# A third buffer for output rows, and an input check finished one turn earlier, in a fused attention and state-space kernel

## The chip, the cores and the metric

The kernel runs on one core of a Trainium2 chip. A core has a matrix engine (TensorE, PE in the profile; its weight loads are listed apart as PEld), a vector engine (VectorE, DVE), a scalar engine for activations and copies (ScalarE, ACT), a general engine (GpSimd, POOL) and a queue for transfers (SyncE, SP). Each works through its own instructions in order, and they wait for one another by semaphores. Matrix products are written to PSUM, from which VectorE and ScalarE read. The metric is the device time of one execution in microseconds; less is better.

## The reference

Two blocks follow each other. The first is a gated linear attention that is written as a recurrence over time: a state of 48 x 48 per head decays by alpha, takes up an outer product of k and v, and is read with q. The second projects the result with `w_in` to a value and a gate, runs a first-order recurrence over the values, multiplies by the gate's SiLU, and projects with `w_out`.

```
state = alpha[:, :, t, :, None] * state + einsum('bhd,bhe->bhde', k[:, :, t], v[:, :, t])
y[:, :, t] = einsum('bhd,bhde->bhe', q[:, :, t], state)          # B=4, H=8, S=768, D=48
x = y.transpose(0, 2, 1, 3).reshape(B, S, H * D)                 # (4, 768, 384)
val, gate = split(x @ w_in)                                      # 512 each
h = a * h + val[:, t]                                            # a = exp(A_log)
out = (silu(gate) * hs) @ w_out                                  # (4, 768, 384), float32
```

The weights and `A_log` arrive as 64-bit floats, and the kernel works in 32-bit floats.

## The kernel before, in words

The sequence is cut into N = 12 groups of 256 steps (three to each of four batches). The function `fast` writes out the order of all instructions by hand: in the loop over turns `n`, a turn projects group n and does the attention of group m = n + 1, while VectorE already prepares later groups. The order of each engine's instructions is the order in which they are written; nothing is rescheduled.

The parts of a turn, with their lines:

- `scores` (L792) and `masks` (L807, L808, L810): products of scaled keys and queries, and their causal mask.
- `values` (L826), `states` (L858), `carried` (L839): what a group's own steps give, the state that it adds, and what earlier states give. `join` (L952 to L957) copies the result out of PSUM and moves it by transfers into `xT`.
- `project(n, cc)` (L976): six products for one quarter of the inner width, three for the value (`pv`), then three for the gate (`pg`); each is carried out as two passes of 256 columns, so a projection is twelve entries in the profile. VectorE then scans `pv` into `hh` (L983), ScalarE makes the gate `sg` from `pg` (L994), and POOL, in the first two turns and in the last one VectorE, multiplies them (L996).
- `output(n)` (L1010): eight products of the gated values with `w_out`, and for each half an eviction by ScalarE into a row `o_sb` (L1004) and a transfer to memory (L1005). Outputs of turns 0 and 1 both fall in turn 1, those of turns 2 to 10 at the end of their own turn, and the last one behind a branch (L1262 to L1270).
- `products` (L661 to L678), advanced step by step by `go`: VectorE's preparation of a later group, with the transposes (L600), the long scans P (L635) and V (L654), and the scaled keys and queries (L619, L610).

Matrix results of `scores` (one half), `project` and `output` live in four PSUM buffers named `mm`, one bank each. Which of the four a tile gets is settled when the program is built: the planner behind the pools simulates the program and gives out a buffer when, by its own estimate, the tile that held it has been read for the last time. It then adds the semaphore waits that the choice requires. `bank("s0")` and its kin are further banks with one buffer each. The rows `o_sb` come from a pool of their own, `rows`, in SBUF.

The kernel has a range check. For inputs outside the range that its method can handle, a second function, `general`, computes the whole again. `check_w(i)` (L567) takes the largest and smallest magnitude of one of six weight parts, `check_end` (L574 to L583) joins these with what was collected on alpha into a column `okc` of 128 ones or zeros, and `check_flag` sums that column by a product with ones on TensorE into the bank `s0` (L587) and makes the flag from it (L589, L590). All engines read the flag at the end of the last turn (L1234) and branch (L1255).

Of the kernel before, what the change touches and what calls it, by code (L numbers as in the profile page):

```python
# [346 lines left out]
def fast(  # L347
# [30 lines left out]
    N = B * NG  # L378
# [67 lines left out]
    NW = 6  # L446
# [491 lines left out]
    for h in range(H):  # L938
        i, e, s = h // 4, h % 4 // 2, h % 2 ^ h // 4
# [23 lines left out]
    def project(n, cc, late=False, between=None):  # L963
        if cc == 0:
            if n == 0:
                fs[n] = [wide[:, k // 2, ds(k % 2 * GC, GC)] for k in range(NI)]
            else:
                fs[n] = [f_last[:, k] for k in range(NI)]
        xT = xTs[n]
        pv, pg = [t[:, 0:GC] for t in bank_pair()]  # L970
        order = [(vg, kk) for vg in range(2) for kk in range(NK)]
        if n == 0 and cc == 0:
            order.sort(key=lambda x: x[1])
        def passes(part):
            for vg, kk in part:
                nc.tensor.matmul((pv, pg)[vg], w_ins[cc][:, kk, vg, :], xT[:, kk, :],  # L976
                                 start=(kk == 0), stop=(kk == NK - 1))

        passes(order[:NK] if between else order)
        hh = p2.tile([C, GC], FP32, tag=f"h{cc}", name="hh")  # L980

        def scan():
            nc.vector.tensor_tensor_scan(  # L983
                out=hh, data0=a_dec[:, cc:cc + 1].to_broadcast([C, GC]), data1=pv,
                initial=prev_h[cc][:, GC - 1:GC] if n % NG else 0.0, op0=ALU.mult, op1=ALU.add)
            prev_h[cc] = hh

        if not late:
            scan()
        if between:  # L990
            between()
            passes(order[NK:])
        sg = gates.tile([C, GC], FP32, tag="sg", name="sg")
        nc.scalar.activation(sg, pg, AF.Silu)  # L994
        engine = nc.vector if n < 2 or n == N - 1 else nc.gpsimd
        f = lambda: engine.tensor_mul(fs[n][cc], sg, hh)  # L996
        return (scan, f) if late else f
# [33 lines left out]
    def go(count):  # L1031
        for _ in range(count):
            next(steps, None)
# [75 lines left out]
    for n in range(N):  # L1109
        m = n + 1  # L1110
        if n == 0:
            V = scan_V(1, P)
            high(1)
            fs_late = [project(n, 0)]
            add_low(1)
            alphas(2)
            scaled_k(1, tk, V)
            scaled_q(1, tq, P)
            low(2)
            fs_late.append(project(n, 1))  # L1120
            convert(2)
            first(m)
            tk = straighten(2, "k")
            P = scan_P(2)
            tq = straighten(2, "q")
            V = scan_V(2, P)
            low(3)
            convert(3)
            load_raw("k", 3, nc.sync)
            junk(1)  # L1130
            def across_and_states():
                values(m, True)
                add_banks(m, states(m))

            f2 = project(n, 2, between=across_and_states)
            nc.scalar.activation(wobits[0][0:1, 0, 0, 0:1], minus[0:1], AF.Relu)
            load_w_out(0, nc.sync)
            alphas(3)
            third(m)
            load_w_out(1, nc.sync)  # L1140
            for name in "qa":
                load_raw(name, 3 + (name == "a"), nc.sync)
            load_v(3, nc.sync)
            for c in range(G):
                scaled_k(2, tk, V, c)
                scaled_q(2, tq, P, c)
        elif n == 1:
            scores(m)
            masks(m)
            h3, f3 = project(0, 3, True)  # L1150
            f2()
            P = scan_P(3)
            h3()
            values(m, True)
            st = states(m)
            add_banks(m, st)
            for f in fs_late:
                f()
            f3()
            f0 = project(n, 0)  # L1160
            convert(4)
            junk(2)
            low(5)
            convert(5)
            f1 = project(n, 1)
            f0()
            tk = plain("k")
            turn("k", tk)
            third(m)
            load_raw("k", 4, nc.sync)  # L1170
            load_v(4, nc.sync)
            f1()
            junk(3)
            V = scan_V(3, P)
            f2 = project(n, 2)
            scaled_k(3, tk, V)
            f2()
            output(0)
            f3 = project(n, 3)
            tq = plain("q")  # L1180
            turn("q", tq)
            load_raw("q", 4, nc.sync)
            scaled_q(3, tq, P)
            f3()
            go(1)
        else:
            if n == 2:
                first(m)
            if n - 1 not in late:
                second(m)  # L1190
                go(4)
            else:
                go(1)
            f0 = project(n, 0)
            f0()
            if n == 2:
                go(2)
            load_raw("k", n + 3, nc.sync)
            load_raw("a", n + 3, nc.sync)
            go(1)  # L1200
            f1 = project(n, 1)
            f1()
            if n - 1 in late:
                second(m)
            if n == 4:
                go(1)
            if n == N - 2:
                for i in range(0, 2):
                    check_w(i)
            go(1)  # L1210
            f2 = project(n, 2)
            f2()
            if n == N - 2:
                check_w(2)
            if n == N - 1:
                check_flag()
            if n != 4:
                go(1)
            load_raw("q", n + 3, nc.sync)
            f3 = project(n, 3)  # L1220
            f3()
            third(m)
            if n not in late:
                first(m + 1)
            elif n > 2:
                go(3)
            load_v(m + 2, nc.sync)
        if n == N - 2:
            for i in range(3, NW):
                check_w(i)  # L1230
            check_end()
        if n == N - 1:
            tc.mark_branch_hint_location("last", hint=0, engines=[mybir.EngineType.PE, mybir.EngineType.Activation, mybir.EngineType.DVE, mybir.EngineType.SP, mybir.EngineType.Pool])
            value = nc.values_load(flag[0:1, 0:1], min_val=0, max_val=1)  # L1234
        if 0 < n < N - 1:
            output(n)
        if n > 1 and n in late:
            first(m + 1)
# [3 lines left out]
@with_exitstack  # L1242
def kernel(ctx: ExitStack, tc: tile.TileContext, *args):
    nc = tc.nc
    out = args[-1]
    C, GC, NI = 128, 256, 4
    B, S, DM = out.shape
    keep = ctx.enter_context(tc.tile_pool(name="keep", bufs=1))
    ps_mm = ctx.enter_context(tc.tile_pool(name="ps_mm", bufs=4, space=bass.MemoryType.PSUM))
    w_outs = [keep.tile([C, 2, DM], FP32, name=f"w_out{i}") for i in range(2)]  # L1250
    f_last = keep.tile([C, NI, GC], FP32, name="f_last")
    rows = ctx.enter_context(tc.tile_pool(name="rows", bufs=2))
    with tc.manual_schedule():
        good = fast(tc, *args, w_outs, f_last, ps_mm, rows)
    with tc.If(good <= 0, preferred_fallthrough_block=True, label="last") as choice:  # L1255
        general(tc, *args, w_outs)
    with choice.Else(), tc.manual_schedule():
        half = DM // 2
        for c, at, size in ((0, 0, DM), (1, 0, half), (1, half, half)):
            o = ps_mm.tile([C, 512], FP32, tag="mm", name="mm")[:, 0:size]  # L1260
            for cc in range(NI):
                nc.tensor.matmul(o, f_last[:, cc, ds(c * C, C)], w_outs[cc // 2][:, cc % 2, ds(at, size)],  # L1262
                                 start=(cc == 0), stop=(cc == NI - 1))
            if not at:
                o_sb = rows.tile([C, DM], FP32, tag="o_sb", name="o_sb")
            if c and not at:
                nc.vector.tensor_copy(out=o_sb[:, 0:half], in_=o)
            else:
                nc.scalar.activation(o_sb[:, ds(at, size)], o, AF.Copy)
            nc.scalar.dma_start(out=out[B - 1, ds(S - GC + c * C, C), ds(at, size)], in_=o_sb[:, ds(at, size)])  # L1270
# [30 lines left out]
```

## Time and profile before

| what | value |
|---|---|
| median of 3 runs | 276.58 us (276.08 to 277.28) |
| the profiled execution | 276.15 us |
| its span, from first to last instruction | 274.4 us |
| TensorE busy | 269.5 us, 98% of the span |
| VectorE busy | 217.7 us, 79% |
| ScalarE busy | 109.6 us, 40% |
| POOL busy | 123.8 us, 45% |
| granted TensorE clock | 1.00 |

A row of a timeline reads: start in us from the span's start, duration, engine, line of the kernel, operation, output <- inputs, shapes, number of instructions; in brackets the idle time of that engine just before, and what ended it. A row of the chain gives start, duration and line of a piece of the work that ended last. A row of the waits reads: who, for whom, us in total, times, longest. A row of groups reads: line, operation, shapes, count, busy time, mean ns of one, idle time of the engine before them. Matrix products are pipelined, so their durations overlap and their spacing is shorter than one duration.

### The profile page before, as it was taken

How to read it: one execution, taken by the hardware profiler on the slowest of the kernel's cores; microseconds unless marked ns; L12 is line 12 of the kernel's file. 1: busy time of each engine (PE TensorE's matmuls, PEld its weight loads, DVE VectorE, ACT ScalarE, POOL GpSimd, SP SyncE). 2: the span in 40 equal slices, each digit the busy share in tenths (PEclk: the TensorE clock that was granted, in tenths of full speed). 3: DMA queues.
4: the chain of work that ended last, by engine and by line, in shares of the span. 5: the costliest groups of instructions: out<-in, count | busy, mean ns of one | idle time of the engine just before them, and what ended most of it. 6: DMA issues, size and time to landing. Idle time of an engine off the chain costs nothing.

```text
span 274.4 us, 9649 instructions
## 1 busy us (share of the span) xinstructions
PE 269.5 (98%) x4060; PEld 216.9 (79%) x4060; DVE 217.7 (79%) x271; ACT 109.6 (40%) x252; POOL 123.8 (45%) x144
## 2 busy tenths in 40 slices
PE   8999999999999999999999999999999999999995
PEld 6988888877788687788688688688687787786874
DVE  6979998996798999694995995996995992179440
ACT  3668766451344333523434424425425415213211
POOL 8122223260137485385384485376366476325000
PEclk9999999999999999999999999999999999999999
DMA  6937985989639686774677595586596501201101
GB/s 188 319 113 221 304 182 160 256 172 230 168 92 227 163 189 152 199 170 116 153 183 155 149 210 136 142 202 144 137 210 146 137 0 36 70 0 42 63 5 60
DMA packets 52303, 41.18 MB, mean 150 GB/s; under 512 B 27392, under 2 KB 50944, under 8 KB 52256
## 3 DMA queue, kind: packets, MB, share of 16 engines
q1 hardware_dynamic: 49328, 37.34, 54.2%
q0 software_dynamic: 1536, 2.20, 2.9%
q10 hardware_dynamic: 1392, 0.99, 1.2%
q8 instruction: 33, 0.54, 0.9%
q14 instruction: 14, 0.11, 0.1%
HBM read 32.54 MB, written 4.72 MB: 136 GB/s over the span
## 4 chain that ended last, share of the span: by engine, by line
PE 91%; DVE 5%; issue 1%; ACT 1%; POOL 1%; DVEq 0%; POOLq 0%; ACTq 0%
PE mm L976 46%; PE mm L1010 21%; PE y L826 4%; PE y L839 4%; PE mm L792 3%; PE s L792 3%; PE s L858 3%; PE mm L1262 2%; DVE P L635 2%; PE mm L701 1%; PE y L773 1%; DVE V L654 1%; POOL w_in L556 1%; PE s L717 1%; DVE Zk L619 0%
## 5 line engine op out<-in xcount | busy, mean ns | idle before, releaser
L976 PE MATMUL mm<-xT,w_in 128*128 128x256 f32 x576 | 129.7, 382 | 0.1
L976 PEld LDWEIGHTS mm<-xT,w_in 128*128 128x128 f32 x576 | 107.9, 190 | 16.2 <-POOL w_in L556 0.4
L1010 PE MATMUL mm<-w_out,f_last 128*128 128x384 f32 x160 | 54.2, 492 | 0.0
L994 ACT ACTIVATE sg<-mm 128x256 f32<-128x256 f32 x48 | 18.4, 383 | 86.1 <-PE mm L976 86.0
L996 POOL TENSOR_TENSOR f_last<-sg,hh 128x256 f32<-128x256 f32 x36 | 33.0, 918 | 33.5 <-ACT sg L994 17.7
L1010 PEld LDWEIGHTS mm<-w_out,f_last 128*128 128x128 f32 x160 | 29.7, 190 | 19.8
L878 POOL TENSOR_TENSOR sum<-sum,dS 128x192 f32<-128x192 f32 x30 | 30.3, 1010 | 21.5 <-ACT dS L866 11.8
L983 DVE TENSOR_TENSOR_SCAN hh<-a_dec,hh,mm 128x256 f32<-128x256 f32 x32 | 23.4, 731 | 16.1 <-PE mm L976 16.1
L635 DVE TENSOR_TENSOR_SCAN P<-al,lower 128x1028 f32<-128x1028 f32 x12 | 31.4, 2618 | 0.5
L654 DVE TENSOR_TENSOR_SCAN V<-al,ends 128x1028 f32<-128x1028 f32 x12 | 28.3, 2360 | 0.4
L955 POOL DMA_DIRECT2D xT<-yst x44 | 22.5, 517 | 12.5 <-ACT yst L952 11.2
L1004 ACT ACTIVATE o_sb<-mm 128x384 f32<-128x384 f32 x22 | 10.8, 490 | 37.3 <-issue 21.2
L810 POOL TENSOR_TENSOR AK<-AK,mask 128x512 f32<-128x512 f32 x9 | 15.2, 1684 | 18.7 <-ACT AK L808 18.7
L807 DVE TENSOR_TENSOR A<-s,mask 128x256 f32<-128x256 f32 x9 | 3.8, 425 | 19.5 <-PE s L792 19.5
L556 POOL TENSOR_TENSOR w_in<-w_in,wr 128x768 int32<-128x768 int32 x4 | 7.3, 1822 | 25.9 <-DVE wr L551 16.1
L600 DVE STREAM_TRANSPOSE k<-raw_k 128x1024 f32<-128x1024 f32 x9 | 18.3, 2035 | 0.0
L600 DVE STREAM_TRANSPOSE q<-raw_q 128x1024 f32<-128x1024 f32 x9 | 18.2, 2021 | 0.0
L600 DVE STREAM_TRANSPOSE al<-raw_a 128x1024 f32<-128x1024 f32 x8 | 16.3, 2038 | 0.0
L619 DVE TENSOR_TENSOR Zk<-k,V 128x1024 f32<-128x1024 f32 (+1 forms) x14 | 16.1, 1150 | 0.1
L826 PEld LDWEIGHTS y<-AK,v 64*64 64x64 f32 x352 | 12.1, 134 | 5.1 <-issue 5.1
L610 DVE TENSOR_TENSOR Zq<-q,P 128x1024 f32<-128x1024 f32 (+1 forms) x14 | 14.8, 1060 | 0.1
L826 PE MATMUL y<-A,v 64*64 64x64 f32 x352 | 14.5, 221 | 0.0
(163 smaller groups left out, 389.7 us busy)
## 6 DMA issues: line engine op xcount, KB each, us to landing
v<-in_v_dram SPq DMA_DIRECT2D x22, 192.0 KB, 3.3
out_dram<-o_sb SPq DMA_DIRECT2D x22, 192.0 KB, 2.2
raw_k<-in_k_dram SPq DMA_DIRECT2D x18, 184.0 KB, 3.7
raw_q<-in_q_dram SPq DMA_DIRECT2D x18, 184.0 KB, 3.8
raw_k<-in_k_dram SPq DMA_DIRECT2D x18, 176.0 KB, 3.9
raw_q<-in_q_dram SPq DMA_DIRECT2D x18, 176.0 KB, 4.0
wbits<-in_moe_w_in_dram SPq DMA_DIRECT2D x8, 384.0 KB, 5.3
raw_a<-in_alpha_dram SPq DMA_DIRECT2D x16, 184.0 KB, 4.9
```

The source lines that it names most:

```text
L600: nc.vector.transpose(out=by_runs(to).rearrange("p h c j -> p h j c"), in_=raws[name][:, 0:4 * ROW].rearrange("p (h j d) -> p h j d", h=4, ...
L635: nc.vector.tensor_tensor_scan(out=P, data0=al[:, 0:4 * GP], data1=lower.rearrange("p h t -> p (h t)"), initial=0.0, op0=ALU.mult, op1=ALU ...
L654: nc.vector.tensor_tensor_scan(out=V[:, ::-1], data0=al[:, 1:4 * GP + 1][:, ::-1], data1=ends.rearrange("p h t -> p (h t)")[:, ::-1], init ...
L792: nc.tensor.matmul(scs[m][c][i][ds(L * h, L), ds(p * (L + D), L + D)], Zk[rows, c, p, ds(h * L, L)], Zq[rows, u, p], start=True, stop=True ...
L826: nc.tensor.matmul(ys[m][i][ds(64 * s, 64), e, ds(c * C + h * L, L)], v_sb[rows, c, 4 * i + p, :], As[i][rows, c, p, :], start=across and ...
L878: nc.gpsimd.tensor_add(Ss[j][:, :, 0:D], Ss[j - 1][:, :, 0:D], part)
L955: engines[n % len(engines)].dma_start(out=xT[to, a], in_=st[rows, i, e])
L976: nc.tensor.matmul((pv, pg)[vg], w_ins[cc][:, kk, vg, :], xT[:, kk, :], start=(kk == 0), stop=(kk == NK - 1))
L983: nc.vector.tensor_tensor_scan(out=hh, data0=a_dec[:, cc:cc + 1].to_broadcast([C, GC]), data1=pv, initial=prev_h[cc][:, GC - 1:GC] if n % ...
L994: nc.scalar.activation(sg, pg, AF.Silu)
L996: f = lambda: engine.tensor_mul(fs[n][cc], sg, hh)
L1010: nc.tensor.matmul(os[c], fs[n][cc][:, ds(c * C, C)], w_outs[cc // 2][:, cc % 2, :], start=(cc == 0), stop=(cc == NI - 1))
```

## The change

Three things are changed. The pool `rows` gets three buffers instead of two. In the last turn but one (n = N - 2 = 10), the reductions of the range check move: four of the six weight parts stand ahead of the turn's first projection, one behind the second, one behind the third, and the end of the check behind the fourth; before, two parts stood behind the second projection, one behind the third, and three with the end of the check behind the attention. The summing product of the check moves from the third projection of the last turn to the end of turn 10, directly in front of that turn's output, and its two VectorE instructions with it.

```
             else:
                 go(1)
+            if n == N - 2:
+                for i in range(4):
+                    check_w(i)
             f0 = project(n, 0)
             f0()
...
             if n == N - 2:
-                for i in range(0, 2):
-                    check_w(i)
+                check_w(4)
             go(1)
             f2 = project(n, 2)
             f2()
             if n == N - 2:
-                check_w(2)
-            if n == N - 1:
-                check_flag()
+                check_w(5)
             if n != 4:
                 go(1)
             load_raw("q", n + 3, nc.sync)
             f3 = project(n, 3)
             f3()
+            if n == N - 2:
+                check_end()
             third(m)
...
         if n == N - 2:
-            for i in range(3, NW):
-                check_w(i)
-            check_end()
+            check_flag()
         if n == N - 1:
...
-    rows = ctx.enter_context(tc.tile_pool(name="rows", bufs=2))
+    rows = ctx.enter_context(tc.tile_pool(name="rows", bufs=3))
```

The built programs hold the same instructions on every engine. On TensorE only the summing product changes its place; on VectorE the check's instructions do; the order on ScalarE, POOL and SP is the same. The semaphore waits differ in more places.

More of the change, by code (lines that the diff above doesn't have):

```diff
@@ L1193, in fast @@
                 go(1)
+            if n == N - 2:
+                for i in range(4):
+                    check_w(i)
             f0 = project(n, 0)
@@ L1207, in fast @@
             if n == N - 2:
-                for i in range(0, 2):
-                    check_w(i)
+                check_w(4)
             go(1)
@@ L1213, in fast @@
             if n == N - 2:
-                check_w(2)
-            if n == N - 1:
-                check_flag()
+                check_w(5)
             if n != 4:
@@ L1221, in fast @@
             f3()
+            if n == N - 2:
+                check_end()
             third(m)
@@ L1228, in fast @@
         if n == N - 2:
-            for i in range(3, NW):
-                check_w(i)
-            check_end()
+            check_flag()
         if n == N - 1:
@@ L1251 @@
     f_last = keep.tile([C, NI, GC], FP32, name="f_last")
-    rows = ctx.enter_context(tc.tile_pool(name="rows", bufs=2))
+    rows = ctx.enter_context(tc.tile_pool(name="rows", bufs=3))
     with tc.manual_schedule():
```

## The prediction

> **What bounds the kernel now.** I read the busy shares first, then the groups of instructions for what TensorE waited, then the chain that ended last, and last the stretches the edit touches, instruction by instruction.
>
> ```profile
> span 274.4 us, 9649 instructions
> ...
> PE 269.5 (98%) x4060; PEld 216.9 (79%) x4060; DVE 217.7 (79%) x271; ACT 109.6 (40%) x252; POOL 123.8 (45%) x144
> ...
> L976 PE MATMUL mm<-xT,w_in 128*128 128x256 f32 x576 | 129.7, 382 | 0.1
> ...
> L1010 PE MATMUL mm<-w_out,f_last 128*128 128x384 f32 x160 | 54.2, 492 | 0.0
> ```
>
> TensorE works for 269.5 of 274.4 us, and its two costliest lines waited 0.1 and 0.0 us in all. No other engine can be made faster to any effect; what counts is whether TensorE gets an instruction more or less, or a wait it does not have now. The chain around the second turn, the place that matters below:
>
> ```profile
> 66.62 5.16 PE mm L1010 x16
> 71.78 0.93 PE s L792 x32
> 72.71 0.77 PE mm L792 x32
> 73.48 5.38 PE mm L976 x24
> 78.85 0.62 PE y L826 x32
> ...
> 86.43 0.47 PE y L839 x32
> 86.90 0.09 issue
> 86.99 1.00 PE s L792 x32
> ```
>
> Every piece is TensorE's own work and starts where the one before ended; the only wait is 0.09 us at 86.90.
>
> **The change, part by part.**
>
> *Third row buffer, for the rows themselves: 0.* It lets an eviction start before the transfer of the row two evictions earlier has landed. The closest two outputs are those of turns 0 and 1, both evicted in turn 1:
>
> ```profile
> 64.97 2.09 SPq L1005 DMA_DIRECT2D out_dram<-o_sb  x2
> 71.22 0.49 ACT L1004 ACTIVATE o_sb<-mm 128x384 f32<-128x384 f32 x1 [4.18 <-PE mm L1010]
> ...
> DMA to landing us min/median/max: 1.6/2.0/4.2
> ```
>
> The first row left at 64.97 and landed at the latest 4.2 us on, at 69.2; its buffer is wanted again at 71.22, and that eviction waited for TensorE's L1010. Elsewhere a whole turn lies between two outputs. So no eviction waits for a row.
>
> *Third row buffer, for the PSUM banks: +2.0.* The diff does not tell this; the built programs do. The four PSUM buffers named mm are given out, when the program is built, in the order in which the planner thinks they come free, and that order changes when two evictions no longer wait for a row. The instructions of turn 2's first projection, with what each waits for (before, then after; the pv group is the first three, the pg group the next three):
>
> ```
> L976 Matmult mm<-xT,w_in_93 128x256 [waits DMAHW0_49,DMASW1_49,DMASW0_49]
> L976 Matmult mm<-xT,w_in_93 128x256 [waits Activation_49]
> L976 Matmult mm<-xT,w_in_93 128x256 x2
> ...
> L976 Matmult mm<-xT,w_in_93 128x256 [waits DMAHW0_49,DMASW1_49,DMASW0_49]
> L976 Matmult mm<-xT,w_in_93 128x256 [waits DVE_49]
> L976 Matmult mm<-xT,w_in_93 128x256 x2
> ```
>
> Before, pg's first matmul waits for ScalarE: the eviction of a row, long over. After, it waits for VectorE, for the count of the scan L983 that reads pv of this same projection: pv and pg have been given one and the same bank (their PSUM addresses are equal, the only such pair among the 163 mm tiles). So pg cannot begin until VectorE has scanned pv. When is that? VectorE's order is unchanged here, and the scan stands behind the long scan P:
>
> ```profile
> 73.53 0.42 DVE L807 TENSOR_TENSOR A<-mm,mask 128x256 f32<-128x256 f32 x1 [0.34 <-PE mm L792]
> 73.87 2.29 DVE L635 TENSOR_TENSOR_SCAN P<-al,lower 128x1028 f32<-128x1028 f32 x1
> 76.07 0.72 DVE L983 TENSOR_TENSOR_SCAN hh<-a_dec,hh,mm 128x256 f32<-128x256 f32 x1
> ```
>
> The mask product, itself waiting for TensorE's L792, ends at 73.9, P runs until 76.1, the scan until 76.07+0.72 = 76.79. TensorE, in its rows, starts pg's first pass (the seventh of the 24) at 74.81:
>
> ```profile
> 74.81 0.38 PE L976 MATMUL mm<-xT,w_in 128*128 128x256 f32 x1
> ...
> 246.93 0.73 POOL L996 TENSOR_TENSOR f_last<-sg,hh 128x256 f32<-128x256 f32 x1 [2.50 <-DVE hh L983]
> ...
> L976 PE MATMUL mm<-xT,w_in x364: 379/379/483, 99.8 to 247.9; 128*128 128x256 f32 x182
> ```
>
> From VectorE's end to the waiter's start no TensorE wait of this kind is in the trace. The nearest row is POOL's at 246.93, behind a scan that ended at 246.05+0.74 = 246.79 (row further down): 0.14. The other end is 0. I take 0.05, as the weight load itself carries the wait and nothing stands before it. A first pass after a stop takes 483 instead of 379 ns, as that row's largest and smallest show: 0.10. The stall is 76.79+0.05-74.81+0.10 = 2.13 us; its ends are 1.98 (nothing for either) and, with P at its slowest, 2.97:
>
> ```profile
> 213.19 3.04 DVE L635 TENSOR_TENSOR_SCAN P<-al,lower 128x1028 f32<-128x1028 f32 x1
> ```
>
> (76.79+0.14-74.81+0.10 = 2.22, and 3.04-2.29 = 0.75 more). What stands behind the held instruction is all of TensorE's queue, so everything later moves by the same amount. VectorE and POOL gain slack, so the 0.09 us at 86.90 goes: net +2.04. The other groups of turn 2 whose waits changed name readers that are over by then: ScalarE's copies of the masks' step (before L858), and a scan that ends at 82.50+0.74 = 83.24 (row below), for pv of the turn's fourth projection. TensorE reaches that one at 80.20+2.7 = 82.9 by the profile of before (the second L976 pair of the turn starts behind L826 and L858, at 78.85+0.62+0.72 = 80.2), and some 2.1 us later, at 85.0, after.
>
> ```profile
> 82.50 0.74 DVE L983 TENSOR_TENSOR_SCAN hh<-a_dec,hh,mm 128x256 f32<-128x256 f32 x1
> ```
>
> *Range check earlier: 0, under cover of TensorE, if the check is in time.* In turn 10 VectorE now does four pairs of reductions ahead of the first scan, one pair behind the second, one behind the third, and the end of the check behind the fourth.
>
> ```profile
> 231.13 0.42 DVE L807 TENSOR_TENSOR A<-mm,mask 128x256 f32<-128x256 f32 x1 [0.34 <-PE mm L792]
> 239.37 0.75 DVE L983 TENSOR_TENSOR_SCAN hh<-a_dec,hh,mm 128x256 f32<-128x256 f32 x1 [7.81 <-PE mm L976]
> 241.96 0.75 DVE L983 TENSOR_TENSOR_SCAN hh<-a_dec,hh,mm 128x256 f32<-128x256 f32 x1 [1.84 <-PE mm L976]
> 242.62 0.93 DVE L567 TENSOR_REDUCE wmax<-wbits 128x1 f32<-128x768 f32 x1
> ...
> 246.05 0.74 DVE L983 TENSOR_TENSOR_SCAN hh<-a_dec,hh,mm 128x256 f32<-128x256 f32 x1
> ...
> 254.20 0.18 DVE L574 TENSOR_SCALAR rok<-ratio 128x48 f32<-128x48 f32 x1
> ...
> 255.10 0.16 DVE L583 TENSOR_REDUCE okc<-ok 128x1 f32<-128x4 f32 x1
> ```
>
> Four reductions take 246.05-242.62 = 3.43, one 0.86. Eight of them fit from 231.55 to 238.4, ahead of the scan at 239.37. TensorE's pace then brings scans every 2.59: 239.37, 241.96, 244.55, 247.14; a pair of 1.72 fits between each two. In turn 10 the last two scans even come earlier than now (the third at 244.55 instead of 246.05), which moves POOL's products forward and nothing on TensorE. The check's end, 254.20 to 255.26, is 1.06 long and would run from 247.8 to 248.9.
>
> *The summing product (L587) in front of the output: -0.2.* It waits for okc, and all of L1010, the output of turn 10, is queued behind it, and behind that turn 11.
>
> ```profile
> 249.81 1.56 PE L1010 MATMUL mm<-w_out,f_last 128*128 128x384 f32 x4
> ...
> 263.01 0.12 PE s L587 x2
> ...
> 260.52 0.38 ACT L994 ACTIVATE sg<-mm 128x256 f32<-128x256 f32 x1 [2.21 <-PE mm L976]
> 263.11 0.38 ACT L994 ACTIVATE sg<-mm 128x256 f32<-128x256 f32 x1 [2.21 <-PE mm L976]
> 266.01 0.38 ACT L994 ACTIVATE sg<-mm 128x256 f32<-128x256 f32 x1 [2.52 <-PE mm L976]
> ```
>
> TensorE gets there at 249.81, 0.9 us after okc; turn 2's shift moves both alike. Where L587 stands now it costs more than its own 0.12: the gates of turn 11 come 2.59 apart without it (260.52 to 263.11) and 2.90 with it (263.11 to 266.01), so 0.31; the weights of L976, else loaded ahead, are loaded in the open behind it. In front of L1010 that load is in the open already, since the small tiles of L839 go before; there I take its own 0.12, with 0.31 as the other end. Net 0.12-0.31 = -0.19 (ends -0.19 and 0). The two VectorE instructions behind it (L589, L590) and the reading of the flag by all engines come some 13 us earlier; nothing waited for them on TensorE, so 0.
>
> **Sum.** +2.13 -0.09 -0.19 = +1.85 us. The profiled execution took 276.15 us (span 274.4), so 278.00; the median of the runs shown is 276.58, 0.43 above it, and I carry the same difference: 278.4, +0.67%. With the ends: 1.98-0.09-0.19 = 1.70 to 2.97, so 278.3 to 279.6, and the runs before spread over 276.08 to 277.28, so about half a microsecond more to either side. What a measurement of this kernel can tell from no change is 0.5%, 1.4 us.
>
> **Rivals.** *The stall is swallowed further on* (the other side: not slower). Place: a later point where TensorE waits for a transfer or another engine in any case; price: the stall up to that point's idle time. From 0.7 us on it would decide against "slower" (1.85-0.7 is under 1.4). Then 276.58-0.19 = 276.4. Against it: after 64 us no wait is put down to TensorE's matmuls at all, and its weight loads show, in the waits from 64 us to the end, only these:
>
> ```profile
> PEld y L826 <- issue: 4.5, 9, 0.5
> PEld y L839 <- issue: 3.0, 9, 0.3
> PEld s L792 <- PE mm L1010: 1.1, 2, 0.5
> ```
>
> They come alike in every turn, at changes of tile shape, with matmuls running meanwhile. Chance 0.08.
>
> *The flag's product becomes the bound.* If one pair of reductions ran past its scan, okc would come 1.7 us later, at 250.6, and L587 would hold the output for 250.6-249.8 = 0.8 us: 278.4+0.8 = 279.2. It decides from 0.9 us of delay on. For it: the gaps between scan and pair are only 0.2 us wide. Chance 0.06.
>
> *The clock falls in the stall.*
>
> ```profile
> 268.00:271.00 3.00, 3.00 (x18) 2.65 (x16) 0.36 (x1) 0.49 (x1) 0.00 (x0) 1.00 0.19 68
> 271.50:274.40 2.90, 0.00 (x0) 0.00 (x0) 0.00 (x0) 0.00 (x0) 0.00 (x0) 1.00 0.11 34
> ```
>
> The seventh figure behind the stretch's length is the granted clock: 1.00 at work, and 1.00 still over 2.9 us without a matmul at the end. A stall of 2 us should leave it. If it halved for one projection of 2.59 us, the time would be 278.4+2.6 = 281.0. Chance 0.04. [...]
>
> *Faster by more than 0.5%*: would need the evictions' waits to be TensorE's, with 3.3 us to win; L1010's 0.0 speaks against it. Chance 0.02.
>
> **Chances and range.** The stall of about 2 us, alone: 0.80, own range 277.6 to 279.6. With the late flag, 0.86 is held by 277.5 to 279.8; the swallowed stall and the fallen clock are left out. Slower by over 0.5% (above 278.0): most of the first case (0.73), the late flag and the clock, 0.83. Within 0.5%: the swallowed stall, and the part of the first that spread hides, 0.15. Faster: 0.02.
>
> **What would show it.** A pause on TensorE of about 2 us at 74.8, ended by VectorE's hh (L983), before the seventh L976 of turn 2; L792 of that turn at about 89.0 instead of 86.99, with no wait before it; L1010 of turn 10 some 2.2 us later than 249.81, the gates of turn 11 all 2.59 apart, L587 right before L1010 with no wait for okc; the clock at 1.00. The prediction is wrong if no pause stands at 74.8, or if the shift shrinks between turns 3 and 10.

## The result, and the profile after

The changed kernel takes 279.29 us in the median of 8 runs (277.55 to 279.95); the kernel before, measured beside it, takes 276.42 us (275.83 to 277.28, 8 runs). The ratio is 1.0091, with a 95% interval of 1.0063 to 1.0119: slower by about 0.9%. The profiled execution of the changed kernel took 279.95 us.

The page of the changed kernel, first its busy shares and the granted clock over 40 slices of the span, then the groups of its two costliest lines:

```profile
span 278.2 us, 9640 instructions
...
PE 271.4 (98%) x4060; PEld 218.2 (78%) x4060; DVE 220.1 (79%) x271; ACT 109.6 (39%) x252; POOL 124.5 (45%) x144
...
PEclk9999999999979999999999999999999999999999
...
L976 PE MATMUL mm<-xT,w_in 128*128 128x256 f32 x576 | 131.4, 386 | 2.0 <-DVE hh L983 1.9
...
L1010 PE MATMUL mm<-w_out,f_last 128*128 128x384 f32 x160 | 54.2, 492 | 0.0
```

Two things are new. The projection L976 now has 2.0 us of idle time in front of it, 1.9 of them ended by VectorE's scan `hh`. And it is busy for 131.4 us where it was busy for 129.7, with the same 576 passes; the twelfth slice of the clock line shows 7 where the kernel before had a 9. So the page shows a wait and, beside it, lost clock.

The waits of TensorE from 64 us to the end (who, line, for whom: us in total, times, longest). For the kernel before, this view has no row for TensorE's matmuls:

```profile
PE mm L976 <- DVE hh L983: 1.9, 1, 1.9
```

The place, in the timeline of the changed kernel, row by row as for the kernel before in the prediction:

```profile
73.99 0.42 DVE L807 TENSOR_TENSOR A<-mm,mask 128x256 f32<-128x256 f32 x1 [0.34 <-PE mm L792]
74.33 2.29 DVE L635 TENSOR_TENSOR_SCAN P<-al,lower 128x1028 f32<-128x1028 f32 x1
76.54 0.72 DVE L983 TENSOR_TENSOR_SCAN hh<-a_dec,hh,mm 128x256 f32<-128x256 f32 x1
77.31 0.48 PE L976 MATMUL mm<-xT,w_in 128*128 128x256 f32 x1 [1.88 <-DVE hh L983]
```

The seventh pass of turn 2's first projection starts 0.05 us after the scan's end (76.54+0.72 = 77.26), 1.88 us after TensorE ran dry, and takes 0.48 us. Note that the mask product stands at 73.99, not at 73.53: this execution is already 0.46 us later when the change first matters.

The windows around the stop (length, then busy time and number of instructions of PE, PEld, DVE, ACT and POOL, granted clock, DMA share, GB/s):

```profile
75.14:78.55 3.41, 1.53 (x8) 1.11 (x7) 3.41 (x3) 0.00 (x0) 2.54 (x1) 1.00 0.01 5
78.55:81.97 3.42, 3.42 (x10) 2.71 (x9) 3.33 (x5) 1.51 (x3) 2.40 (x1) 0.50 0.50 126
81.97:85.00 3.03, 3.03 (x105) 2.51 (x104) 3.03 (x4) 0.85 (x3) 1.06 (x2) 1.00 1.03 225
```

TensorE works for 1.53 us of the first stretch. In the next one, which begins 1.2 us after the stop is over, the clock is 0.50 for 3.4 us: ten passes have a part in it, where at 2.59 us for twelve there would be some sixteen. Then it is 1.00 again.

The chain that ended last, of the changed kernel around turn 2 and from the end of turn 10, and behind it the rows of the kernel before that the prediction did not show:

```profile
77.31 5.84 PE mm L976 x18
83.15 0.62 PE y L826 x32
...
90.73 0.47 PE y L839 x32
91.20 0.77 PE s L792 x32
91.97 0.77 PE mm L792 x32
92.73 4.39 PE mm L1010 x13
...
253.16 0.70 PE y L839 x48
253.86 0.12 PE s L587 x2
253.98 5.36 PE mm L1010 x16
259.34 10.36 PE mm L976 x48
269.70 5.19 PE mm L1262 x24
```

```profile
88.76 5.36 PE mm L1010 x16
...
249.88 5.36 PE mm L1010 x16
255.24 7.77 PE mm L976 x36
263.01 0.12 PE s L587 x2
263.13 2.79 PE mm L976 x12
265.92 5.19 PE mm L1262 x24
```

These rows give the whole difference of the two profiled executions, stage by stage:

| stage | before | after | difference |
|---|---|---|---|
| up to the mask product of turn 2 | 73.53 | 73.99 | +0.46 |
| from there to pg's first pass | 74.81 | 77.31 | +2.50-0.46 = +2.04 |
| from there to L826 (18 passes) | 78.85-74.81 = 4.04 | 83.15-77.31 = 5.84 | +1.80 |
| from there to L1010 of turn 2 | 88.76-78.85 = 9.91 | 92.73-83.15 = 9.58 | -0.33 |
| from there to L1010 of turn 10 | 249.88-88.76 = 161.12 | 253.98-92.73 = 161.25 | +0.13 |
| from there to L1262 | 265.92-249.88 = 16.04 | 269.70-253.98 = 15.72 | -0.32 |

The sum is +3.78, and the executions differ by 279.95-276.15 = 3.80. Of the +1.80, 0.10 is the long first pass and 1.70 the halved clock (3.41 us at half speed are 1.71 us of work). A second profile of the changed kernel, from an execution that kept its clock, bears this out: there the eighteen passes take 4.15 us, 0.11 more than before, in its chain:

```profile
76.39 4.15 PE mm L976 x18
```

The 0.46 stands ahead of the place where the change first matters and is no part of it; the same amount and more lies between executions of one kernel.

The 8 runs fall into two groups by the mean granted clock of the execution: 277.55, 277.95 and 278.06 at 0.998 to 1.000, and 279.15, 279.43, 279.75, 279.75 and 279.95 at 0.994. The lower mean is the one stretch: half of 3.41 us in 278 is 0.006. The median of all lies in the second group.

### The profile page after: what moved, and what is told of

Its sections match the earlier page's. It is cut to its first block, busy times and chain, and to the rows that moved or that the text cites. A ratio compares the mean times of both kernels' runs of the same rounds, so it can differ in the third digit from the quotient of the medians.

```text
span 278.2 us, 9640 instructions
## 1 busy us (share of the span) xinstructions
PE 271.4 (98%) x4060; PEld 218.2 (78%) x4060; DVE 220.1 (79%) x271; ACT 109.6 (39%) x252; POOL 124.5 (45%) x144
## 4 chain that ended last, share of the span: by engine, by line
PE 89%; DVE 5%; issue 2%; DMA 1%; ACT 1%; POOL 1%; DVEq 0%; ACTq 0%; POOLq 0%
PE mm L976 45%; PE mm L1010 21%; PE y L826 4%; PE y L839 4%; PE mm L792 3%; PE s L792 3%; PE s L858 3%; DVE P L635 2%; PE mm L1262 2%; PE mm L701 1%; DMA raw_a<-in_alpha_dram 1%; DVE V L654 1%; POOL w_in L556 1%; DVE Zk L619 0%; PE s L717 0%
## 5 line engine op out<-in xcount | busy, mean ns | idle before, releaser
L976 PE MATMUL mm<-xT,w_in 128*128 128x256 f32 x576 | 131.4, 386 | 2.0 <-DVE hh L983 1.9
L976 PEld LDWEIGHTS mm<-xT,w_in 128*128 128x128 f32 x576 | 109.0, 192 | 18.9 <-DVE hh L983 2.3
L1010 PE MATMUL mm<-w_out,f_last 128*128 128x384 f32 x160 | 54.2, 492 | 0.0
L1010 PEld LDWEIGHTS mm<-w_out,f_last 128*128 128x128 f32 x160 | 29.7, 190 | 19.7
L878 POOL TENSOR_TENSOR sum<-sum,dS 128x192 f32<-128x192 f32 x30 | 31.3, 1044 | 21.7 <-ACT dS L866 12.1
L983 DVE TENSOR_TENSOR_SCAN hh<-a_dec,hh,mm 128x256 f32<-128x256 f32 x32 | 23.5, 734 | 13.4 <-PE mm L976 13.1
L635 DVE TENSOR_TENSOR_SCAN P<-al,lower 128x1028 f32<-128x1028 f32 x12 | 31.2, 2598 | 0.5
L826 PEld LDWEIGHTS y<-AK,v 64*64 64x64 f32 x352 | 12.1, 134 | 5.1 <-issue 5.1
L610 DVE TENSOR_TENSOR Zq<-q,P 128x1024 f32<-128x1024 f32 (+1 forms) x14 | 14.8, 1057 | 0.1
L839 PEld LDWEIGHTS y<-Zq,sum 48*64 48x64 f32 x656 | 11.8, 134 | 3.6 <-issue 3.5
```

What stands on the lines that cost most here:

```text
L635: nc.vector.tensor_tensor_scan(out=P, data0=al[:, 0:4 * GP], data1=lower.rearrange("p h t -> p (h t)"), initial=0.0, op0=ALU.mult, op1=ALU ...
L826: nc.tensor.matmul(ys[m][i][ds(64 * s, 64), e, ds(c * C + h * L, L)], v_sb[rows, c, 4 * i + p, :], As[i][rows, c, p, :], start=across and ...
L839: nc.tensor.matmul(ys[m][i][ds(64 * s, 64), e, ds(u * L, L)], Ss[j][rows, p, :], Zqs[m % 2][rows, u, p, D:], start=False, stop=True, skip_ ...
L878: nc.gpsimd.tensor_add(Ss[j][:, :, 0:D], Ss[j - 1][:, :, 0:D], part)
L983: nc.vector.tensor_tensor_scan(out=hh, data0=a_dec[:, cc:cc + 1].to_broadcast([C, GC]), data1=pv, initial=prev_h[cc][:, GC - 1:GC] if n % ...
L1010: nc.tensor.matmul(os[c], fs[n][cc][:, ds(c * C, C)], w_outs[cc // 2][:, cc % 2, :], start=(cc == 0), stop=(cc == NI - 1))
```

## The experiments

The theory after the first profile of the changed kernel: the third row buffer makes the planner give pv and pg of turn 2's first projection one bank; the stop of TensorE behind VectorE's scan costs 2.1 us, and in some executions it also makes the clock fall, for 1.7 us more; the moved check brings back 0.2 us. The rivals: the loss has to do with the moved check; or with the third row itself, its memory or its transfers; or the clock's fall has another cause than the stop.

**The third buffer alone.** The kernel before with one edit:

```
-    rows = ctx.enter_context(tc.tile_pool(name="rows", bufs=2))
+    rows = ctx.enter_context(tc.tile_pool(name="rows", bufs=3))
```

> The kernel before with the third row buffer alone. Theory (the third buffer makes the planner give pv and pg of turn 2's first projection one PSUM bank, TensorE stands for about 2 us until VectorE's scan L983 has read pv, and in part of the executions the clock then halves for 3.4 us): a pause of TensorE of 1.9 us ended by DVE hh L983, 276.4 + 2.14 - 0.32 = 278.2 us where the granted clock is 1.000, some 1.6 us more, 279.8, where it is 0.994. Rival (the third buffer is idle, the moved check costs the time): no pause, 276.4 us.

Measured: 278.19 us (277.51 to 279.88, 6 runs), ratio 1.0076 (1.0051 to 1.0100). Its waits of TensorE have the same single row as the changed kernel, to the tenth:

```profile
PE mm L976 <- DVE hh L983: 1.9, 1, 1.9
```

Two executions had the clock at 0.994 (279.74, 279.88), four at 1.000 (277.51 to 278.25). The stop and the loss come with the number of the pool's buffers, without any move of the check.

**The moved check alone.** The changed kernel with the pool set back:

```
-    rows = ctx.enter_context(tc.tile_pool(name="rows", bufs=3))
+    rows = ctx.enter_context(tc.tile_pool(name="rows", bufs=2))
```

> The change with two row buffers: only the range check and its summing product are moved. Theory: no pause anywhere, the clock at 1.000, the gates of turn 11 all 2.59 us apart, L587 0.12 us in front of L1010, so 276.4 - 0.2 = 276.2 us, not to be told from before. Rival (the moved check costs the time): 278 us or more, with TensorE waiting for okc or in turns 10 and 11.

Measured: 275.93 us (275.38 to 276.15, 11 runs), ratio 0.9987 (0.9977 to 0.9997). No wait of TensorE's matmuls from 64 us on, clock at 0.998 or more in all 11. The gates of the last turn, all four, in its timeline:

```profile
257.47 0.38 ACT L994 ACTIVATE sg<-mm 128x256 f32<-128x256 f32 x1 [2.11 <-PE mm L976]
260.06 0.38 ACT L994 ACTIVATE sg<-mm 128x256 f32<-128x256 f32 x1 [2.21 <-PE mm L976]
262.65 0.38 ACT L994 ACTIVATE sg<-mm 128x256 f32<-128x256 f32 x1 [2.21 <-PE mm L976]
265.24 0.38 ACT L994 ACTIVATE sg<-mm 128x256 f32<-128x256 f32 x1 [2.21 <-PE mm L976]
```

They are 2.59 us apart throughout, where the kernel before had one step of 2.90. So the moved check is worth a gain of 0.13%, some 0.4 us by the ratio, with an interval that holds the 0.19 us of the chain. It is the better half of the change, by itself.

**Three buffers and two banks.** The changed kernel, but the second row of turn 1's output goes into a tile that is dead by then, instead of into a buffer of `rows`. By the theory the planner then gives pv and pg two banks again, with three buffers and the moved check kept:

```
-            o_sb = rows.tile([C, DM], FP32, tag="o_sb", name="o_sb")
+            if n == 1 and c == 1:
+                o_sb = wide[:, 1, 0:DM]
+            else:
+                o_sb = rows.tile([C, DM], FP32, tag="o_sb", name="o_sb")
```

> The changed kernel, three row buffers and the moved check, but the second row of turn 1's output goes to the tile wide, which is free by then, so that in the planner's estimate no eviction waits and pv and pg of turn 2's first projection get two banks. Theory (only the shared bank costs): no pause, the clock at 1.000, 276.2 us, the same as before. Rival (the third buffer or the moved check costs something of its own): 277 us or more.

Measured: 276.34 us (275.49 to 276.83, 12 runs), against 276.30 us (275.65 to 279.48, 17 runs) of the kernel before beside it; ratio 0.9987 (0.9958 to 1.0016), no wait of TensorE's matmuls, clock at 0.998 or more in all 12. No view here shows the bank of pg; that the stop is gone speaks for it. The pool of three with its memory is there and costs nothing that this measurement can tell; what costs is the shared bank.

Two of those 17 executions of the kernel before stand apart: 279.45 us at a clock of 1.000, and 279.48 at 0.994. So now and then an execution is 3 us longer, and a stretch of clock can be lost, without the stop in turn 2; in the 41 executions of the kernel before beside the experiments, a stretch of clock was lost this once. Where it was lost is not known, as no profile of it exists.

**VectorE's scan of pv earlier.** The changed kernel with VectorE's steps of turn 2 put off by one place, so that the scan of pv (L983) stands ahead of the long scan P (L635):

```
-            else:
+            elif n > 2:
                 go(1)
...
             if n == 2:
-                go(2)
+                go(3)
```

> The changed kernel with VectorE's scan of pv (L983) put ahead of the long scan P (L635) in turn 2; the two share a bank as before. Theory: the scan then starts when pv is done, some 0.2 us after its last pass started plus that pass, so pg starts about 1.0 us late instead of 2.0; P comes 1.2 us later, which may hold L792 of that turn by some 0.3 us. 276.4 + 1.1 - 0.2 + 0 to 0.3 = 277.3 to 277.6 us, and the clock 1.000 in every execution, since a stop of 1 us is too short to take it. Rival (any stop can take the clock): some executions at 0.994 and about 279.0 us.

Measured: 277.46 us (277.17 to 277.72, 5 runs), ratio 1.0042 (1.0028 to 1.0055), clock at 0.998 or more in all 5. First its timeline, then its waits:

```profile
75.38 0.75 DVE L983 TENSOR_TENSOR_SCAN hh<-a_dec,hh,mm 128x256 f32<-128x256 f32 x1 [1.05 <-PE mm L976]
76.04 2.27 DVE L635 TENSOR_TENSOR_SCAN P<-al,lower 128x1028 f32<-128x1028 f32 x1
76.18 1.13 PE L976 MATMUL mm<-xT,w_in 128*128 128x256 f32 x4 [0.84 <-DVE hh L983]
```

```profile
PE mm L976 <- DVE hh L983: 1.2, 2, 0.8
```

The stop follows the scan: with P behind it, it is 0.84 us, which is the scan's own length (0.75) and 0.04 and 0.05 us ahead of it and behind it. A second one of 0.34 us (1.2-0.84), at 84.46, appears at the turn's fourth projection, where VectorE's steps of this turn now all stand one place later. So more than half of the stop (1.04 of 1.88 us) was P's place in VectorE's order. What is left is the shared bank's own price: VectorE waits for pv (the 1.05 us in its row), and pg waits for VectorE.

**The stop filled with products of zeros.** The changed kernel, with eight passes of a product of zeros into the unused bank `y` between the pv and the pg group of turn 2's first projection. They add work and leave nothing out:

```
+        if n == 2 and cc == 0:
+            passes(order[:NK])
+            keep_warm(4, 256)
+            passes(order[NK:])
+        else:
+            passes(order[:NK] if between else order)
```

> The changed kernel with four products of zeros (eight passes of 256 columns, 8 x 0.216 = 1.73 us) put on TensorE between pv and pg of turn 2's first projection, where it stands still; pg still waits for the scan. Theory (the pause itself costs 2.1 us, and its idleness the clock): the same start of pg, the granted clock 1.000 in every execution, 278.0 us, with none near 279.6. Rival (the clock falls for another reason, or zeros do not count as work): most executions at a clock of 0.994 and 279.6 us as in the changed kernel.

Measured: 277.83 us (277.50 to 279.10, 6 runs), ratio 1.0056 (1.0042 to 1.0070), and the clock at 0.998 or more in all 6, also in the slowest, whose head was 1.3 us late. Its timeline, and two stretches of 3.41 us, the one that holds the filled stop and the one behind it:

```profile
74.72 1.56 PE L976 MATMUL mm<-xT,w_in 128*128 128x256 f32 x6
76.12 1.90 PE L773 MATMUL y<-const-float32-0.0 128*128 128x256 f32 x8
78.17 0.70 PE L976 MATMUL mm<-xT,w_in 128*128 128x256 f32 x2
```

```profile
75.81:79.22 3.41, 3.27 (x16) 2.54 (x15) 3.41 (x3) 0.06 (x1) 2.73 (x1) 1.00 0.01 3
79.22:82.64 3.42, 3.42 (x39) 2.78 (x41) 3.33 (x4) 1.80 (x4) 0.73 (x1) 1.00 0.44 110
```

The delay is as long as before (pg starts at 78.17, 1.89 us after pv's last pass has ended at 74.72+1.56 = 76.28), but TensorE isn't idle in it, and the clock stays at 1.00. The two stretches begin and end where this trace's own records of the clock put the borders of such stretches (how is shown further down): unfilled, the 1.89 us would have lain whole in the first of them, as the 1.88 us did where the clock fell. The kernel with the stop lost clock in 7 of 15 executions (5 of 8 of the changed kernel, 2 of 6 of the third buffer alone, none of one further run below); if the fill did nothing, six without a loss would come with a chance of (8/15)^6 = 2%. So here the clock fell with TensorE idle for 1.88 us, and not with the same wait of 1.89 us filled. The stop without the clock is worth 1.0056 (1.0042 to 1.0070), and the 0.67% of the prediction's sum lies in that interval.

**A longer stop.** The changed kernel with one more VectorE instruction in turn 2, which clears a dead tile ahead of the projection, so that the scan comes later; then the same with half the tile:

```
+            if n == 2:
+                nc.vector.memset(wide, 0.0)
             f0 = project(n, 0)
```

> The changed kernel with a memset of the dead tile wide (1440 columns, about 1.4 us by the 1.15 us that VectorE takes for products over 1024 columns) on VectorE between the long scan P and the scan of pv, so that the stop of TensorE lasts about 3.4 us instead of 1.9. Theory (the clock falls when enough of some fixed stretch of 3.4 us is idle, and where the stretch begins varies from execution to execution): now it falls in every execution, the granted clock never 1.000, and the time is 278.0 + 1.4 + 1.7 = 281.1 us, up to 1.7 us more where two stretches are lost. Rival (the fall is chance and has nothing to do with the length): clock 1.000 in a third of the executions, as in the changed kernel, and 279.4 us there.

Measured: stop 3.30 us; 281.06 us (278.76 to 283.11, 6 runs), ratio 1.0122 (1.0069 to 1.0175; taken without the 283.11). The clock was 1.000 in three executions, 0.994 in two and 0.988 in one. That it would be lost in every execution was wrong. In the profiled one, it was kept; its windows on both sides of 79.19:

```profile
75.78:79.19 3.41, 1.92 (x26) 1.27 (x18) 2.82 (x4) 1.29 (x4) 2.26 (x1) 1.00 0.19 66
79.19:82.60 3.41, 1.60 (x7) 1.44 (x8) 3.41 (x3) 0.00 (x1) 0.76 (x1) 1.00 0.00 0
82.60:86.00 3.40, 3.40 (x81) 2.82 (x82) 3.31 (x6) 1.90 (x4) 0.73 (x1) 1.00 0.61 148
```

This asked for another idea: what counts is how the stop lies on a fixed grid of stretches of 3.413 us, the length of the record at 0.5 in the trace of the changed kernel. The borders of such a grid can be had from the trace's own records of the granted clock, which give start, length and value in us. For the changed kernel, up to the end of its span:

```
start    length   granted
  6.87    71.68   1.0
 78.55     3.41   0.5
 81.97   197.97   1.0
```

The lengths are whole numbers of 3.413 (71.68 is 21 of them, 197.97 is 58; in the trace of the kernel before, the record at 1.0 is 269.65 us long, 79 of them), so every border is taken as the first record's start plus a multiple. In the longer stop's profile a border (79.19) cuts the stop into 1.49 and 1.81 us. To test this, there are three further runs with such stops and one of the changed kernel: the half tile (`memset(wide[:, 0], 0.0)`, stop 2.55 us), the whole tile once more, the changed kernel once more, and the half tile once more.

> The changed kernel with a memset of half of the dead tile wide (720 columns) on VectorE between the scan P and the scan of pv: a stop of TensorE of about 2.6 us. Theory (the clock works in stretches of 3.413 us that lie on a grid fixed before the kernel starts, and it halves for the next stretch when a stretch has had at least some 1.85 us of stop in it: 1.88 in one stretch lost it in two profiles, 1.49 and 1.81 in two neighbouring ones kept it): the clock is lost exactly where the grid leaves 1.85 us or more of the stop in one stretch, 278.0 + 0.7 = 278.7 us where it is kept and 280.4 where not. Rival (chance): the profile shows a lost clock with less, or a kept one with 1.9 us or more in one stretch.

> The same kernel as the one with the stop of 3.3 us, once more, to see where its grid lies. Theory: as above; kept only where the stop is split so that neither part reaches 1.85 us, lost everywhere else; 278.8 us kept, 280.5 to 281.1 with one stretch lost, 283 with two. Rival (chance): kept although 1.9 us or more lie in one stretch.

> The changed kernel as it is, looked at again for where the grid lies. Theory: a stop of 1.88 us; the clock is lost if it lies inside one stretch, kept if a border of the grid cuts it; 277.9 or 279.6 us. Rival (chance): kept although the stop lies inside one stretch.

> The kernel with the stop of 2.6 us, a second look. Theory and rival as for the first look at it: lost where 1.85 us or more of the stop lie in one stretch of the grid, kept where less.

Measured: the half tile 280.15 us (278.95 to 280.33, 4 runs), ratio 1.0118 (1.0089 to 1.0146), three executions at 0.994 and one at 1.000; the whole tile again 279.86 us (278.92 to 281.74, 4 runs), ratio 1.0127 (1.0075 to 1.0179), two at 1.000, one each at 0.994 and 0.988; the changed kernel again 277.33 us at 1.000; the half tile again 277.92 us at 1.000. Every stop in front of pg that a profile shows, on the grid of its own execution:

| kernel | stop | its parts in one stretch and the next | clock in the stretch behind |
|---|---|---|---|
| changed kernel | 75.43 to 77.31 | 1.88 | 0.50 |
| third buffer alone | 75.04 to 76.92 | 1.88 | 0.50 |
| half tile | 75.15 to 77.70 | 2.55 | 0.50 |
| whole tile again | 74.46 to 77.75 | 1.17, 2.12 | 0.50 |
| whole tile | 77.70 to 81.00 | 1.49, 1.81 | 1.00 |
| half tile again | 74.44 to 76.98 | 1.54, 1.00 | 1.00 |
| changed kernel again | 74.51 to 76.39 | 1.29, 0.59 | 1.00 |
| scan of pv earlier | 75.34 to 76.18 | 0.84 | 1.00 |

The same kernel on both sides, in windows on the grid: the whole tile again, whose 2.12 us lie in the second stretch, and the changed kernel again, whose 1.88 us are cut:

```profile
75.63:79.04 3.41, 1.29 (x6) 1.16 (x7) 3.16 (x4) 0.00 (x0) 1.07 (x1) 1.00 0.00 0
79.04:82.46 3.42, 3.42 (x10) 2.71 (x9) 3.33 (x5) 1.51 (x3) 2.50 (x1) 0.50 0.55 125
```

```profile
72.38:75.79 3.41, 2.13 (x34) 1.47 (x26) 3.07 (x4) 1.49 (x4) 2.06 (x1) 1.00 0.25 88
75.79:79.20 3.41, 2.81 (x13) 2.51 (x14) 3.32 (x5) 1.22 (x2) 1.69 (x2) 1.00 0.00 0
```

The last four runs came out as the theory had it. In all eight, the clock fell where at least 1.88 us of one stretch were idle (TensorE busy 1.53 us or less) and stayed where it was at most 1.81 us (busy 1.60 or more). The total length of the stop didn't decide it: 3.30 us kept the clock once, 1.88 us lost it. The ends of two traces agree. In the kernel before and in the changed kernel, the last product ends at 271.10 and 274.88; the stretch that holds this end (to 272.64 and 276.53) has 1.54 and 1.65 us idle, and the clock behind it is still 1.0; the next stretch is idle whole (3.41 us), and the record behind that one says 0.5.

The shares that follow are estimates from these lengths. If the grid lay at random against the kernel, the stop of 1.88 us would fall whole into one stretch in (3.41-1.88)/3.41 = 45% of the executions; 7 of 15 were seen. The stop of 2.55 us would keep the clock in about a third, taking 1.85 us, a value between the 1.81 that kept it and the 1.88 that lost it, as the border between the two; 2 of 5 were seen. The stop of 3.30 us would keep it in about 12%; 5 of 10 were seen. But the profiles don't show the grid at random: in the first seven of the table the stop begins 0.20 to 0.63 us behind a border in three, and 1.87 to 2.24 us behind one in the other four. So these shares are rough, the 12% above all, since a stop of 3.30 us is kept only if it begins some 1.6 to 2.0 us behind a border. Why the grid lies in two places is not shown, nor when it is fixed, which the first of the four expectations puts ahead of the kernel's start; and for executions without a profile neither the phase nor the parts are known.

One thing stays open. By these numbers a stop of 3.30 us should not cost two stretches, as it can't put 1.85 us into each of two; yet two of its 10 executions had a clock of 0.988. The second stretch may have been lost elsewhere, as in the one execution of the kernel before; no profile shows either of the two.

## Why the prediction was right, point by point

The direction, the cause and its place came out as predicted: slower, by the shared bank, at the seventh pass of turn 2's first projection. The median, 279.29, lies 0.9 us above the predicted 278.4 and inside the range of 277.5 to 279.8. This closeness is partly luck: the median holds a lost stretch of clock that the sum does not have; the predicted number stands between two groups of executions (277.55 to 278.06, and 279.15 to 279.95), and no run gave it.

- *The rows themselves, 0.* Right: three buffers with two banks took 276.34 us, ratio 0.9987 (0.9958 to 1.0016).
- *The stall, +2.13.* Right: 2.04 of waiting and 0.10 of the long first pass. The source of the 0.10 was misread: in the trace of before, which has no such stop, the passes of 483 ns stand behind products of another line (L858 and L792 mostly); that a pass behind a stop takes as long was seen only now, at 77.31. The 0.05 us from the scan's end to the pass was measured as 0.05, P ran its 2.29, and the third buffer alone gives the same row of waits.
- *The 0.09 us at 86.90 that goes.* Mis-sized: it was -0.33. The wait of 0.09 goes, and the L792 behind it runs in 0.77 instead of 1.00 us (rows at 91.20 and 86.99). The prediction took the wait and left out that the instructions behind it had been drawn out too. In the profile of the scan of pv earlier, in which pg is held up too, the wait is gone as well, and L792 runs in 0.77. VectorE's product Zq (L610), which L792 reads, ends 0.15 us ahead of L792 in the kernel before (85.63+1.21 = 86.84) and 3.31 us ahead of it in the changed one (86.69+1.20 = 87.89). So L792 probably ran on the heels of Zq; no run separates this.
- *The range check, 0.* Right. `okc` is ready at 252.65+0.16 = 252.81, TensorE asks for it at 253.86, so 1.05 us are to spare (0.9 predicted).

```profile
243.35 0.75 DVE L983 TENSOR_TENSOR_SCAN hh<-a_dec,hh,mm 128x256 f32<-128x256 f32 x1 [0.93 <-PE mm L976]
...
252.65 0.16 DVE L583 TENSOR_REDUCE okc<-ok 128x1 f32<-128x4 f32 x1
...
254.02 0.15 DVE L589 TENSOR_SCALAR fl<-s 1x1 f32<-1x1 f32 x1 [1.22 <-PE s L587]
```

These are VectorE's rows of turn 10 of the changed kernel: the first scan of the turn still waits 0.93 us for TensorE behind the eight reductions, as the sum of 8 times 0.86 had it.

- *L587 in front of the output, -0.19.* Right in both terms: +0.13 where it stands now, -0.32 where it stood.
- *The upper end, and the price of a swallowed stall.* Two sums are off, with no weight in the result. The upper end of 2.97 leaves out the 0.09 that the sum takes off; with it, 2.88. And a swallowed stall would have decided against "slower" from 0.45 us on (1.85-1.4), not from 0.7.
- *Swallowed stall.* It did not happen. From L1010 of turn 2 to that of turn 10 the shift neither grows nor shrinks but for L587's 0.13.
- *Late flag.* It did not happen, by the 1.05 us.
- *The clock falls in the stall.* This is the step that failed. The prediction gave it a chance of 0.04, from one row (2.9 us without a matmul at the end of the span, clock 1.00), and a price of 2.6 us. It happened in 5 of the 8 runs and cost 1.70 in the profiled one; that the low clock would last for one projection of 2.59 us was the author's estimate, and the record at 0.5 lasts 3.41. The row was no evidence: in the changed kernel the stretch with the stop still has 1.00 and the one behind it 0.50, and behind the end of the span there was no next one to be seen. (The records of the kernel before go on for 0.42 us behind the first stretch without a product, 272.64 to 276.05, with the span over at 274.4: they say 0.5.) From that row the stop of about 2 us had been taken as harmless; the measurement decides against it, as a stretch that was 55% idle (1.88 of 3.41) was followed by 0.50.

The terms as measured, without the clock: 2.14-0.33-0.19 = +1.62, on 276.42 this is 278.0; the three runs at 0.998 to 1.000 took 277.55 to 278.06. With 1.70 more it is 279.7; the five at 0.994 took 279.15 to 279.95. The likeliest case and the rival with 0.04 were, in truth, about equally frequent.

The version to keep is the moved check with two row buffers: 275.93 us, ratio 0.9987 (0.9977 to 0.9997) to the kernel before, within the half per cent that counts as no change.

## What to carry to other kernels

Where a planner gives out buffers, the size of a pool can change another pool's choices: after such an edit, compare the semaphore waits of the built programs, since two groups that followed each other on TensorE in one bank stopped it here for 1.88 us, until the reader of the first was done. Price a stop of TensorE with the clock in mind: the one of 1.88 us cost 1.70 us more in the stretch behind it in the profiled execution, and the clock was lost in 7 of 15 executions and not in the others, so look at the granted clock of every run before a median is explained. Where a stop can't be avoided, it can be filled: with products of zeros in it the clock was kept here (0.998 or more in 6 of 6 executions).

## What the runs showed of the hardware that was not expected

- The granted clock stood at 0.50 for a stretch of 3.41 us and went back to 1.00. The records of the clock last 71.68, 3.41 and 197.97 us in the changed kernel and 269.65 us in the kernel before: 21, 1, 58 and 79 times 3.413. On the grid that these lengths give, a stretch with 1.88 us or more of idle TensorE was followed by one stretch at 0.50, one with 1.81 us or less was not (eight stops in front of pg, and the ends of two traces). In the profile of the changed kernel, the lost stretch cost 1.70 us of TensorE's work.
- The changed kernel has two groups of times, 277.55 to 278.06 us at a clock of 0.998 to 1.000 and 279.15 to 279.95 at 0.994. In its two profiles the stop of 1.88 us lies whole in one stretch where the clock was lost, and is cut into 1.29 and 0.59 where it was kept. The stop of 3.30 us had a mean clock of 0.988 in two of 10 executions, 283.11 and 281.74 us: about two stretches. One stop of that length doesn't explain both, by the numbers above.
- The head of the kernel varies from one execution to the next: the stop of the whole-tile kernel began at 77.70 us in one profile and at 74.46 in another. Such shifts of some 3 us stand in single times, of the kernel before too (279.45 us at a clock of 1.000), and have nothing to do with the change.
